# A two-stage kernel (gated linear attention, then a feed-forward layer): low parts and scaled queries on GpSimd, high parts on VectorE

## The chip, the cores and the metric

One core of one Trainium2 chip. The time is the device time of one execution in microseconds; 582.28 us is the median of three executions before the change (582.17, 582.28 and 584.62). The engines are named as in the profile: PE is TensorE's matmuls, PEld its weight loads, DVE VectorE, ACT ScalarE, POOL GpSimd, and SP the engine that issues the loads and stores.

## What is computed

A recurrence over 768 steps for 4 batches of 8 heads of 48 channels, and on its output (3072 tokens of 384 channels) a two-layer feed-forward block with 2048 hidden channels and an activation built from softplus and erf:

```
state = zeros(B, H, D, D)
for t in range(S):
    state = alpha[t][..., None] * state + k[t] outer v[t]
    y[t]  = q[t] @ state
x = y as (B*S, H*D)
h  = x @ w_in
sp = max(h, 0) + log1p(exp(-|h|))
g  = h * erf(sp)
out = g @ w_out
```

## The kernel before

The recurrence is done in 24 chunks of 64 steps for two batches at once. Of a chunk, `ld` issues the loads of alpha, k, q and v on SP; `a1` is the running product A of alpha (one scan on VectorE); `a2` makes 1/A with a logarithm and an exponential on ScalarE and refines it on VectorE; `a3` multiplies: K = k/A (line 175) and the scaled queries Q = q*A (lines 178 to 180), both on VectorE; `a4` transposes K and forms the scores on TensorE; `a5` forms the chunk's output and the new state T on TensorE and VectorE, and puts the output, split in a high and a low part, into x_hi and x_lo. The input tiles raw_a, raw_q and raw_k exist once, so the next `ld` waits until the current chunk has read them.

The feed-forward part works in 12 blocks of 256 tokens, a block being two chunks. The 2048 hidden channels are cut into four groups `g`, and each group into two halves. `H_g_half` is the first product (18 matmuls, TensorE), copied to `hs` by ScalarE. `U` is a tanh, `L1` three logarithms and exponentials, `G` a Gelu on ScalarE, `L2` and `Z` two long VectorE operations each; after `Z` the tile `hs` holds the gated values. `U` and `G` need one table of functions on ScalarE and `L1` and `a2` another; the steps `GELU` and `LN` load them (line 115).

`O_g_half` is the second product (lines 347 to 370). All large products are made in pairs of fp32r numbers: a value is split into a high part, rounded to fp32r, and a low part, the rest. `O` makes the high part `gh` of 512 gated values per partition (on VectorE for the first half of the even groups, 24 in all; on ScalarE for the other 72), then on VectorE the low part `gl` = value - gh, and adds up three products, gh with w_out's high part, gh with its low part, and gl with its high part, for two slices of hidden channels and two halves of the tokens: 12 matmuls into the two accumulators `acc`. `gh` and `gl` have two buffers each. `out` copies the accumulators and stores them.

The weights come in 12 slices of w_in (`wi_n`) and 16 of w_out (`wo_n`); they arrive as 64-bit floats, and VectorE and ScalarE make an fp32 number of each in three VectorE steps and one ScalarE step, and then split it (lines 379 to 404).

The order of all this is written out by hand in three lists of steps (lines 27 to 41): `START` once, for the weights, the first six chunks, the first block's `H` to `L2` and the first `H` of the next block; `ORDER` eleven times, once for each further block, with the second half (`G`, `Z`, `O`) of the block before (`@-1`) and the first `H` of the next (`@1`) woven in; `TAIL` for the second half of the last block. The tile framework orders each engine's queue from these lists by its own priorities; every engine works its queue in order.

Of the kernel before, what the change touches and what calls it, by code (L numbers as in the profile page):

```python
# [15 lines left out]
AF = mybir.ActivationFunctionType  # L16
# [7 lines left out]
LNEXP, GELU = "natural_log_exp_and_others", "gelu_and_others"  # L24
# [2 lines left out]
START, ORDER, TAIL = (  # L27
    z.split()
    for z in (
# [10 lines left out]
    )  # L40
)

# [2 lines left out]
def gla_moe(ctx: ExitStack, tc: tile.TileContext, q, k, v, alpha, w_in, w_out, out):  # L45
    nc = tc.nc
# [3 lines left out]
    P = NI * TC  # L50
    B, H, S = M * NI, 2 * NP, CPB * TC
    W = NP * NI * TC
    NT, DM = out.shape
# [4 lines left out]
    NF = FF // P  # L58
    GT = 4
# [27 lines left out]
    for i in range(NI):  # L87
        half = maskn[i * TC : (i + 1) * TC]
        nc.gpsimd.affine_select(
            out=half, in_=half, pattern=[[1, TC]], compare_op=ALU.is_ge, fill=0.0, base=0, channel_multiplier=-1  # L90
# [16 lines left out]
    wo_hi = const.tile([P, NF, DM], F32R, name="wo_hi")  # L107
    wo_lo = const.tile([P, NF, DM], F32R, name="wo_lo")
# [25 lines left out]
    class Chunk:  # L134
# [37 lines left out]
        def a3(self):  # L172
            flat = "p a i t -> p (a i t)"
            w = self.K.rearrange(flat)
            nc.vector.tensor_tensor(out=w, in0=self.rk.rearrange(flat), in1=w, op=ALU.mult)
            self.Q = at.tile([P, NP, NI, TC], F32, name="Q", tag="Q")
            flat = "p a i t -> p (a i) t"
            nc.vector.tensor_tensor(
                out=self.Q.rearrange(flat), in0=self.rq.rearrange(flat), in1=self.A[:, :, 1:], op=ALU.mult
            )  # L180

# [77 lines left out]
    class Moe:  # L259
# [87 lines left out]
        def O(self, g, half):  # L347
            if g == 0 and half == 0:
                self.acc = [self.pl.acc.tile([P, 512], F32, name="acc", tag="acc") for _ in range(2)]
            sl = slice(half * 512, (half + 1) * 512)  # L350
            gg = self.hs[g][:, sl]
            gh = self.pl.gp.tile([P, 2, TB], F32R, name="gh", tag="gh")
            gl = self.pl.gp.tile([P, 2, TB], F32R, name="gl", tag="gl")
            ghf = gh.rearrange("p a t -> p (a t)")
            if half == 0 and g % 2 == 0:
                nc.vector.tensor_copy(out=ghf, in_=gg)  # L356
            else:
                nc.scalar.activation(ghf, gg, AF.Copy)  # L358
            nc.vector.tensor_tensor(  # L359
                out=gl.rearrange("p a t -> p (a t)"), in0=gg, in1=ghf.bitcast(F32), op=ALU.subtract  # L360
            )
            for u in range(2):
                f = g * GT + half * 2 + u
                for tt in range(2):
                    ts = slice(tt * P, (tt + 1) * P)
                    for n, (gt, wt) in enumerate(((gh, wo_hi), (gh, wo_lo), (gl, wo_hi))):
                        nc.tensor.matmul(  # L367
                            out=self.acc[tt][:, :DM], lhsT=gt[:, u, ts], rhs=wt[:, f, :],
                            start=f == 0 and n == 0, stop=f == NF - 1 and n == 2,
                        )  # L370

        def out(self):
            for tt in range(2):
# [154 lines left out]
    for i in range(1, NBLK):  # L528
# [6 lines left out]
        out=top[:, 0:2], in_=flags.rearrange("p n two -> p two n"), op=ALU.max, axis=mybir.AxisListType.X  # L535
# [67 lines left out]
```

## Time and profile before

| | before |
|---|---|
| median of three executions | 582.28 us |
| the profiled execution, whole | 582.33 us |
| its span, first to last instruction | 580.4 us |
| mean granted clock of TensorE | 0.969 |
| matmuls | 7386 |
| low parts gl, VectorE (line 359) | 96, mean 686 ns |
| high parts gh, ScalarE (line 358) | 72, mean 625 ns |
| high parts gh, VectorE (line 356) | 24, mean 419 ns |
| scaled queries Q, VectorE (line 178) | 24, mean 684 ns |

An instruction's duration in the profile reaches beyond the point at which the next one may start; on a full engine the distance from start to start is what it costs. In rows of the timeline the first number is the start and the second the duration, both in us. In rows of groups the last part is the total of the group in us, the mean of one in ns, and the idle time of the engine just ahead of it with what ended it. In rows of waits stand the total, the number of times and the longest, in us.

### The profile page before, as it was taken

What the parts mean: (1) busy time and instruction counts of PE and PEld (TensorE: products, weight loads), DVE (VectorE), ACT (ScalarE), POOL (GpSimd) and SP (SyncE); (2) the same over time, 40 slices, a digit from 0 to 9 for tenths busy, and PEclk for the clock granted to TensorE, in tenths of its full rate; (3) what the DMA queues carried; (4) which work ended last, traced back from release to release, by engine and by line L of the source; (5) the groups of instructions that cost most, each with busy time, mean ns of one, the idle gap of its engine ahead of it and who ended that gap; (6) DMA issues with size and microseconds to landing.
All of it is one profiled execution on the core that took longest, in us unless ns stands there. A gap on an engine that the chain in (4) does not pass through costs nothing.

```text
span 580.4 us, 16926 instructions
## 1 busy us (share of the span) xinstructions
PE 519.5 (90%) x7386; PEld 496.0 (85%) x7386; DVE 483.6 (83%) x688; ACT 468.6 (81%) x704; POOL 2.4 (0%) x16
## 2 busy tenths in 40 slices
PE   0588687499999999999999999999999999999584
PEld 0486686488989999999999999999999999999584
DVE  6779969999999979969789699699699698594970
ACT  4446799579999799699699798797896996989911
POOL 1000000000000000000000000000000000000000
PEclk9999799789999999999999999999999999999878
DMA  6575633522412222212202312221211100000000
GB/s 194 177 230 168 203 91 107 178 86 63 128 28 61 76 55 62 64 52 75 88 25 65 88 32 72 75 61 43 73 62 44 53 8 30 1 29 1 28 0 33
DMA packets 36370, 43.64 MB, mean 75 GB/s; under 512 B 21952, under 2 KB 25024, under 8 KB 36288
## 3 DMA queue, kind: packets, MB, share of 16 engines
q1 hardware_dynamic: 36288, 42.48, 24.3%
q8 instruction: 60, 0.98, 0.7%
q14 instruction: 22, 0.18, 0.1%
HBM read 37.75 MB, written 4.72 MB: 73 GB/s over the span
## 4 chain that ended last, share of the span: by engine, by line
PE 69%; DVE 15%; ACT 9%; issue 3%; DMA 2%; SPq 0%; ACTq 0%; DVEq 0%
PE acc L367 29%; PE ph L310 29%; PE py L226 4%; PE pS L198 3%; DVE wbuf L401 2%; DVE s L342 2%; ACT s L326 2%; PE pu L237 1%; PE pn L187 1%; DVE wbuf L404 1%; DVE A L156 1%; DVE t L334 1%; DVE w L335 1%; DVE hs L343 1%; ACT hs L315 1%
## 5 line engine op out<-in xcount | busy, mean ns | idle before, releaser
L310 PE MATMUL ph<-x_hi,wi_hi 128*128 128x256 f32 x576 | 166.9, 290 | 7.5 <-ACT wi_hi L379 4.8
L310 PE MATMUL ph<-x_lo,wi_hi 128*128 128x256 f32 x576 | 164.0, 285 | 0.0
L310 PE MATMUL ph<-x_hi,wi_lo 128*128 128x256 f32 x576 | 163.7, 285 | 0.3 <-DVE wi_lo L380 0.2
L367 PE MATMUL acc<-wo_hi,gh 128*128 128x384 f32 x384 | 133.2, 347 | 16.4 <-DVE gh L356 16.4
L367 PE MATMUL acc<-wo_hi,gl 128*128 128x384 f32 x384 | 131.4, 346 | 2.0 <-DVE gl L359 1.9
L367 PE MATMUL acc<-wo_lo,gh 128*128 128x384 f32 x384 | 131.0, 341 | 0.0
L310 PEld LDWEIGHTS ph<-x_hi,wi_hi 128*128 128x128 f32 x576 | 111.4, 194 | 10.1 <-ACT wi_hi L379 5.1
L359 DVE TENSOR_TENSOR gl<-hs,gh 128x512 fp32r<-128x512 f32 x96 | 64.9, 686 | 58.4 <-ACT gh L358 57.6
L310 PEld LDWEIGHTS ph<-x_hi,wi_lo 128*128 128x128 f32 x576 | 111.5, 194 | 1.0 <-DVE wi_lo L380 0.8
L310 PEld LDWEIGHTS ph<-x_lo,wi_hi 128*128 128x128 f32 x576 | 111.0, 193 | 0.5 <-DVE x_lo L275 0.3
L367 PEld LDWEIGHTS acc<-wo_hi,gh 128*128 128x128 f32 x384 | 73.8, 192 | 18.0 <-issue 8.7
L315 ACT ACTIVATE hs<-ph 128x512 f32<-128x512 f32 x96 | 56.3, 590 | 39.3 <-PE ph L310 38.1
L367 PEld LDWEIGHTS acc<-wo_hi,gl 128*128 128x128 f32 x384 | 72.7, 191 | 7.4 <-DVE gl L359 7.0
L367 PEld LDWEIGHTS acc<-wo_lo,gh 128*128 128x128 f32 x384 | 73.7, 192 | 0.0
L334 DVE TENSOR_TENSOR t<-s,w 128x1024 f32<-128x1024 f32 x48 | 58.5, 1218 | 1.9 <-ACT w L328 1.4
L335 DVE SCALAR_TENSOR_TENSOR w<-t,w 128x1024 f32<-128x1024 f32 x48 | 58.4, 1216 | 0.3
L358 ACT ACTIVATE gh<-hs 128x512 fp32r<-128x512 f32 x72 | 44.9, 625 | 16.3 <-PE acc L367 12.5
L343 DVE SCALAR_TENSOR_TENSOR hs<-s,hs 128x1024 f32<-128x1024 f32 x48 | 57.9, 1215 | 0.1
L342 DVE TENSOR_TENSOR s<-s,w 128x1024 f32<-128x1024 f32 x48 | 57.5, 1215 | 0.4 <-ACT s L338 0.4
L326 ACT ACTIVATE s<-s,fixed 128x1024 f32<-128x1024 f32 x48 | 54.6, 1141 | 0.0
L321 ACT ACTIVATE s<-hs 128x1024 f32<-128x1024 f32 x48 | 49.7, 1055 | 1.6 <-DVE wbuf L398 0.9
L328 ACT ACTIVATE w<-w 128x1024 f32<-128x1024 f32 x48 | 50.4, 1051 | 0.3
(62 smaller groups left out, 715.1 us busy)
## 6 DMA issues: line engine op xcount, KB each, us to landing
raw_v<-in_v_dram SPq DMA_DIRECT2D x24, 448.0 KB, 3.7
wst<-in_moe_w_in_dram SPq DMA_DIRECT2D x12, 512.0 KB, 5.7
wst<-in_moe_w_out_dram SPq DMA_DIRECT2D x16, 384.0 KB, 3.7
raw_a<-in_alpha_dram SPq DMA_DIRECT2D x48, 96.0 KB, 2.9
raw_k<-in_k_dram SPq DMA_DIRECT2D x48, 96.0 KB, 2.2
raw_q<-in_q_dram SPq DMA_DIRECT2D x48, 96.0 KB, 2.3
out_dram<-o SPq DMA_DIRECT2D x24, 192.0 KB, 1.9
```

The lines of the kernel that those rows point to most:

```text
L310: nc.tensor.matmul(out=o, lhsT=wt[:, kt, fs], rhs=xt[:, kt, :], start=n == 0, stop=n == 3 * KT - 1)
L315: nc.scalar.activation(self.hs[g][:, sl], ph, AF.Copy)
L321: tab(nc.scalar.activation(self.s[g], self.hs[g], AF.Tanh, scale=-0.5))
L326: tab(nc.scalar.activation(s, s, AF.Ln, scale=0.5 - 2.0**-24, bias=bhalf))
L328: tab(nc.scalar.activation(w, w, AF.Exp, scale=-1.0))
L334: nc.vector.tensor_tensor(out=t, in0=s, in1=w, op=ALU.mult)
L335: nc.vector.scalar_tensor_tensor(out=w, in0=t, scalar=2.0, in1=w, op0=ALU.add, op1=ALU.mult)
L342: nc.vector.tensor_tensor(out=s, in0=s, in1=w, op=ALU.mult)
L343: nc.vector.scalar_tensor_tensor(out=h, in0=s, scalar=RT2 / 2, in1=h, op0=ALU.subtract, op1=ALU.mult)
L358: nc.scalar.activation(ghf, gg, AF.Copy)
L359: nc.vector.tensor_tensor(out=gl.rearrange("p a t -> p (a t)"), in0=gg, in1=ghf.bitcast(F32), op=ALU.subtract)
L367: nc.tensor.matmul(out=self.acc[tt][:, :DM], lhsT=gt[:, u, ts], rhs=wt[:, f, :], start=f == 0 and n == 0, stop=f == NF - 1 and n == 2,)
```

## The change

The scaled queries of `a3` and the low parts of `O` are made by GpSimd. All 96 high parts are made by VectorE, none by ScalarE. In `O` the eight products with the high part come first and the four with the low part last. The three lists of steps are written anew.

```diff
             self.Q = at.tile([P, NP, NI, TC], F32, name="Q", tag="Q")
-            nc.vector.tensor_tensor(
+            nc.gpsimd.tensor_tensor(
                 out=self.Q.rearrange(flat), in0=self.rq.rearrange(flat), in1=self.A[:, :, 1:], op=ALU.mult
             )
...
-            if half == 0 and g % 2 == 0:
-                nc.vector.tensor_copy(out=ghf, in_=gg)
-            else:
-                nc.scalar.activation(ghf, gg, AF.Copy)
-            nc.vector.tensor_tensor(
+            nc.vector.tensor_copy(out=ghf, in_=gg)
+            nc.gpsimd.tensor_tensor(
                 out=gl.rearrange("p a t -> p (a t)"), in0=gg, in1=ghf.bitcast(F32), op=ALU.subtract
             )
-            for u in range(2):
-                f = g * GT + half * 2 + u
-                for tt in range(2):
-                    ts = slice(tt * P, (tt + 1) * P)
-                    for n, (gt, wt) in enumerate(((gh, wo_hi), (gh, wo_lo), (gl, wo_hi))):
-                        nc.tensor.matmul(
-                            out=self.acc[tt][:, :DM], lhsT=gt[:, u, ts], rhs=wt[:, f, :],
-                            start=f == 0 and n == 0, stop=f == NF - 1 and n == 2,
-                        )
+            for gt, wts in ((gh, (wo_hi, wo_lo)), (gl, (wo_hi,))):
+                for u in range(2):
+                    f = g * GT + half * 2 + u
+                    for tt in range(2):
+                        for wt in wts:
+                            nc.tensor.matmul(
+                                out=self.acc[tt][:, :DM], lhsT=gt[:, u, tt * P : (tt + 1) * P], rhs=wt[:, f, :],
+                                start=f == 0 and wt is wo_hi and gt is gh, stop=f == NF - 1 and gt is gl,
+                            )
```

Of the lists, the beginning of the one for a further block:

```diff
-        "GELU a1_0 G_0@-1 G_1@-1 Z_0@-1 H_3_0 G_2@-1 U_0 H_3_1 Z_1@-1 O_0_0@-1 U_2 O_0_1@-1 O_1_0@-1 G_3@-1 U_1 "
+        "GELU H_3_0 U_1 G_1@-1 U_0 H_3_1 G_3@-1 Z_1@-1 G_0@-1 U_2 Z_0@-1 O_0_0@-1 a1_0 G_2@-1 O_0_1@-1 Z_2@-1 "
```

Lines behind line 358 stand three earlier in the changed kernel: the cast on VectorE is line 355, the low part line 356, the output product line 364.

VectorE's queue in the third block, from the state's update to the second of the two chunks' K, before:

```order
L178 TENSOR_TENSOR Q<-raw_q,A 128x512
L255 TENSOR_TENSOR T<-T,A 128x8x48
L156 SCALAR_TENSOR_TENSOR A<-raw_a,lower 128x520
L178 TENSOR_TENSOR Q<-raw_q,A 128x512
L359 TENSOR_TENSOR gl<-hs,gh 128x512 x2
L169 TENSOR_TENSOR K<-A,r 128x512
L359 TENSOR_TENSOR gl<-hs,gh 128x512
L170 SCALAR_TENSOR_TENSOR K<-K,r 128x512
L175 TENSOR_TENSOR K<-raw_k,K 128x512
L356 CAST gh<-hs 128x512
L359 TENSOR_TENSOR gl<-hs,gh 128x512
```

The same place in the changed kernel, VectorE:

```order
L255 TENSOR_TENSOR T<-T,A 128x8x48
L156 SCALAR_TENSOR_TENSOR A<-raw_a,lower 128x520
L355 CAST gh<-hs 128x512 x3
L169 TENSOR_TENSOR K<-A,r 128x512
L170 SCALAR_TENSOR_TENSOR K<-K,r 128x512
L334 TENSOR_TENSOR t<-s,w 128x1024
L355 CAST gh<-hs 128x512
L175 TENSOR_TENSOR K<-raw_k,K 128x512
```

And GpSimd's queue in the changed kernel, from its first query on (before, it has no work after the constants of the start):

```order
L178 TENSOR_TENSOR Q<-raw_q,A 128x512 x7
L356 TENSOR_TENSOR gl<-hs,gh 128x512 x5
L178 TENSOR_TENSOR Q<-raw_q,A 128x512
L356 TENSOR_TENSOR gl<-hs,gh 128x512 x3
L178 TENSOR_TENSOR Q<-raw_q,A 128x512
L356 TENSOR_TENSOR gl<-hs,gh 128x512 x2
```

Queries and low parts have left VectorE for GpSimd's queue, where seven queries stand ahead of the first low part; casts stand in VectorE's queue where low parts stood.

TensorE's queue at one whole `O`, before:

```order
L367 MATMUL acc<-wo_hi,gh 128x384
L367 MATMUL acc<-wo_lo,gh 128x384
L367 MATMUL acc<-wo_hi,gl 128x384
L367 MATMUL acc<-wo_hi,gh 128x384
L367 MATMUL acc<-wo_lo,gh 128x384
L367 MATMUL acc<-wo_hi,gl 128x384
```

and in the changed kernel:

```order
L364 MATMUL acc<-wo_hi,gh 128x384
L364 MATMUL acc<-wo_lo,gh 128x384
L364 MATMUL acc<-wo_hi,gh 128x384
L364 MATMUL acc<-wo_lo,gh 128x384
L364 MATMUL acc<-wo_hi,gh 128x384
L364 MATMUL acc<-wo_lo,gh 128x384
L364 MATMUL acc<-wo_hi,gh 128x384
L364 MATMUL acc<-wo_lo,gh 128x384
L364 MATMUL acc<-wo_hi,gl 128x384 x4
```

The four products with the low part have moved behind all eight with the high part (of the order before, half an `O` is shown; the other half is the same).

ScalarE's queue in the last block, from the load of the logarithms' table on, before (s and w are the tiles of `L1`, o is the output's copy):

```order
L115 ACT_TABLE_LOAD
L358 ACTIVATE gh<-hs 128x512
L326 ACTIVATE s<-s,fixed 128x1024
L358 ACTIVATE gh<-hs 128x512
L327 ACTIVATE w<-s 128x1024
L326 ACTIVATE s<-s,fixed 128x1024
L358 ACTIVATE gh<-hs 128x512
L328 ACTIVATE w<-w 128x1024
L327 ACTIVATE w<-s 128x1024
L326 ACTIVATE s<-s,fixed 128x1024
L358 ACTIVATE gh<-hs 128x512
L328 ACTIVATE w<-w 128x1024
```

and in the changed kernel, to the end of the core's work:

```order
L115 ACT_TABLE_LOAD
L326 ACTIVATE s<-s,fixed 128x1024 x2
L327 ACTIVATE w<-s 128x1024 x2
L328 ACTIVATE w<-w 128x1024 x2
L326 ACTIVATE s<-s,fixed 128x1024 x2
L327 ACTIVATE w<-s 128x1024 x2
L328 ACTIVATE w<-w 128x1024 x2
L115 ACT_TABLE_LOAD
L338 ACTIVATE s<-s 128x1024
L372 ACTIVATE o<-acc 128x384
L338 ACTIVATE s<-s 128x1024 x3
L372 ACTIVATE o<-acc 128x384 x3
```

The casts have left ScalarE's queue, and the first output copy stands behind the second table load instead of ahead of it.

18 rows, old and new, of the table RT2 are left out of this document.

## The prediction

> **What bounds the kernel now.** I read the busy line of the page first, then the busy times by stage, then the waits of TensorE.
>
> ```profile
> PE 519.5 (90%) x7386; PEld 496.0 (85%) x7386; DVE 483.6 (83%) x688; ACT 468.6 (81%) x704; POOL 2.4 (0%) x16
> ...
> 0.00:80.00 80.00, 50.65 (x913) 45.69 (x914) 62.14 (x116) 45.38 (x85) 2.41 (x16) 0.96 0.60 186
> 80.00:115.00 35.00, 22.22 (x489) 19.90 (x488) 33.26 (x56) 29.60 (x50) 0.00 (x0) 0.89 0.40 125
> 115.00:164.00 49.00, 46.88 (x635) 43.63 (x636) 48.46 (x77) 44.47 (x69) 0.00 (x0) 0.94 0.30 88
> 164.00:520.00 356.00, 355.82 (x5094) 344.51 (x5094) 304.98 (x403) 316.01 (x461) 0.00 (x0) 1.00 0.18 53
> 520.00:545.00 25.00, 24.86 (x164) 24.05 (x162) 16.53 (x19) 22.04 (x28) 0.00 (x0) 1.00 0.02 9
> 545.00:580.40 35.40, 19.03 (x96) 18.24 (x96) 18.22 (x22) 11.09 (x15) 0.00 (x0) 0.78 0.07 25
> ```
>
> The columns of a stage are its length, the busy time of PE, PEld, DVE, ACT and POOL, the granted clock and the DMA share. The whole-span shares (90, 83, 81%) hide three different kernels. From 164 to 520 us TensorE is busy 355.82 of 356 us: there it is the limit, and nothing taken from VectorE or ScalarE shortens those 356 us. From 80 to 115 us VectorE is busy 33.26 of 35 us while TensorE has 22.22: VectorE is the limit. From 115 to 164 us both are nearly full (48.46 and 46.88 of 49). After 545 us TensorE has 19.03 of 35.4 us and both others are half idle: that is a chain.
>
> ```profile
> DVE gl L359 <- ACT gh L358: 57.6, 26, 7.1
> ...
> PE acc L367 <- DVE gh L356: 16.4, 2, 8.6
> ```
>
> So the time has two handles: how early TensorE becomes full (about 164 us), and how long it stands still at the end. The second row shows TensorE's two long waits for a high part, 16.4 us together; one is before the first output product at 115 us, the other (8.6) in the tail. The 57.6 us in which VectorE waits for ScalarE's high parts lie mostly under a full TensorE and are worth nothing by themselves.
>
> **The start.** The steps from one start to the next on a busy VectorE are the price of an instruction there:
>
> ```profile
> 113.41 0.55 DVE L380 TENSOR_TENSOR wo_lo<-wbuf,wo_hi 128x384 fp32r<-128x384 f32 x1
> 113.88 0.55 DVE L404 SCALAR_TENSOR_TENSOR wbuf<-wbuf 128x384 int32<-128x384 int32 x1
> 114.35 0.35 DVE L398 TENSOR_SCALAR wbuf<-wst 128x384 int32<-128x384 int32 x1
> 114.62 0.42 DVE L356 CAST gh<-hs 128x512 fp32r<-128x512 f32 x1
> 114.95 0.55 DVE L401 SCALAR_TENSOR_TENSOR wbuf<-wbuf 128x384 int32<-128x384 int32 x1
> 115.42 0.55 DVE L380 TENSOR_TENSOR wo_lo<-wbuf,wo_hi 128x384 fp32r<-128x384 f32 x1
> ...
> 161.52 0.42 DVE L356 CAST gh<-hs 128x512 fp32r<-128x512 f32 x1
> ...
> 298.37 0.69 DVE L359 TENSOR_TENSOR gl<-hs,gh 128x512 fp32r<-128x512 f32 x1
> 298.97 1.22 DVE L335 SCALAR_TENSOR_TENSOR w<-t,w 128x1024 f32<-128x1024 f32 x1
> ...
> 323.29 0.68 DVE L178 TENSOR_TENSOR Q<-raw_q,A 128x512 f32<-128x512 f32 x1
> 323.89 1.22 DVE L343 SCALAR_TENSOR_TENSOR hs<-s,hs 128x1024 f32<-128x1024 f32 x1
> ```
>
> A high-part cast costs VectorE 0.33 us (114.62 to 114.95), a low part 0.60 (298.37 to 298.97), a scaled query 0.60 (323.29 to 323.89). The row at 161.52 is the first cast of the second block: from the products behind it on, TensorE is full. Ahead of it VectorE's order holds 9 queries, 8 low parts and 2 casts; in the changed order, ahead of the first cast of that block, it holds none, none and 8. That is -9 x 0.60 - 8 x 0.60 + 6 x 0.33 = **-8.2 us** of VectorE's work, in a stretch where VectorE was full for the last 80 us of it.
>
> TensorE may not be able to take all of this, since it also waits at the first output product (cast at 114.62). Ahead of that cast 6 queries go (-3.6), but one more slice of w_out stands there (0.47 three times and 0.27, +1.7): -1.9 us. Between the two casts TensorE had 2.1 us of idle time to give back (49 less 46.88), so this path gives at least 1.9 + 2.1 = 4.0. The new start order can move the 17.9 us in which VectorE is idle in the first 80 us either way; the last slice of w_in comes earlier in VectorE's order, which speaks for earlier. I take **-6.0 us**, between 4.0 and 8.2.
>
> **The steady part** I cost at nothing. Per block ScalarE loses 6 casts, VectorE loses 8 low parts and 2 queries and gains 6 casts; the cover is TensorE's 355.82 of 356. TensorE's own work is the same matmuls in another order:
>
> ```profile
> 306.39 0.34 PE L367 MATMUL acc<-wo_lo,gh 128*128 128x384 f32 x1
> 306.56 0.34 PE L367 MATMUL acc<-wo_hi,gl 128*128 128x384 f32 x1
> 306.74 0.34 PE L367 MATMUL acc<-wo_hi,gh 128*128 128x384 f32 x1
> 306.91 0.34 PE L367 MATMUL acc<-wo_lo,gh 128*128 128x384 f32 x1
> ```
>
> Every step is 0.17 us, whether the next matmul keeps the accumulator (hi, lo, low) or changes it (306.56 to 306.74), so the new order costs nothing. It buys cover: eight products with the high part, 8 x 0.17 = 1.4 us, now stand ahead of the first that needs the low part.
>
> **What GpSimd's part costs** no row shows. The nearest ones:
>
> ```profile
> L128 POOL MEMSET T<- 128x512 f32 x1 | 0.5, 524 | 0.0
> ...
> masks.py:199 POOL TENSOR_SCALAR_AFFINE_SELECT ident<-ident 128x128 f32<-128x128 f32 x1 | 0.3, 292 | 0.1
> masks.py:197 POOL MEMSET ident<- 128x128 f32 x1 | 0.2, 204 | 0.3 <-POOLq L562 0.3
> ```
>
> Writing 512 elements takes 0.52 us: the lower bound. Reading one operand of 128 adds 292 - 204 = 88 ns, so two operands of 512 add 8 x 88 = 0.70: **1.23 us**, my estimate. The upper bound is the same with the reading at twice that price, 1.93 us. At 1.23 us a low part fits inside the 1.4 us of cover even if its cast ends only just before the products begin, and TensorE spends 12 x 0.17 = 2.1 us on each piece, so even six pieces in a row leave GpSimd time; at 1.93 us it still keeps pace but each first piece could wait 0.5 us. Two buffers let the cast and the low part run a piece ahead. A new wait stands behind each cast on TensorE (all its later work queues behind the first low product) and one on VectorE (a cast waits until TensorE has freed a high-part buffer, with the next block's work behind it); the second takes the place of the 57.6 us row, and is hidden by the same full TensorE. On GpSimd a query ahead of low parts can hold them up while it waits for its load. The reload of raw_q now waits on GpSimd, and what SP issues behind it waits too; the DMA share of 0.18 in the steady stage is the cover.
>
> The Trainium skill, "GPSIMD Engine Reference", section Performance versus the Vector engine, gives 4497 ns for a two-input add of 2048 elements; a quarter of it is an estimate of 1.12 us, which would change no term here.
>
> **The tail.**
>
> ```profile
> 529.48 1.28 ACT L115 ACT_TABLE_LOAD   x1
> 530.77 0.63 ACT L358 ACTIVATE gh<-hs 128x512 fp32r<-128x512 f32 x1
> 531.31 1.14 ACT L326 ACTIVATE s<-s,fixed 128x1024 f32<-128x1024 f32 x1
> ...
> 540.73 0.62 ACT L358 ACTIVATE gh<-hs 128x512 fp32r<-128x512 f32 x1
> 541.25 1.05 ACT L328 ACTIVATE w<-w 128x1024 f32<-128x1024 f32 x1
> ...
> 545.77 1.28 ACT L115 ACT_TABLE_LOAD   x1
> ```
>
> ```profile
> 544.67 0.19 PE L541 MATMUL pf<-fixed,count 128*1 128x1 f32 x2
> 553.46 0.66 PE L367 MATMUL acc<-wo_hi,gh 128*128 128x384 f32 x1 [8.59 <-DVE gh L356]
> ```
>
> In the last block ScalarE is full from the table load at 529.48 to the one at 545.77, and TensorE runs dry at 544.67 because the gated values come 8.6 us later. Of those 16.3 us six are casts of 0.52 to 0.54 (530.77 to 531.31, 540.73 to 541.25), 3.2 us, and one an output copy that the changed order puts behind the load. TensorE's part up to there is the same. What comes next, VectorE's chain from the last logarithm to the first cast, holds six long operations in both orders. So **-3.2 us**; the bounds are -1.6 (half of it, if ScalarE's steps, now in pairs of equal ones, wait for each other) and -4.0 (with the output copy). The low parts on GpSimd (1.23 against TensorE's 2.1 per piece) do not slow the eight pieces that follow.
>
> **Sum**, against the profiled execution's own 582.33 us (span 580.4 and 1.93 around it; the median of the runs shown is 582.28, so no correction): 582.3 - 6.0 - 3.2 = **573.1 us**. Its own range, from the bounds of both terms, is 570 to 577, and 567 if the start order also fills VectorE's early gaps.
>
> **Rivals.** (1) *GpSimd stops VectorE.* If VectorE's operations with two SBUF inputs and GpSimd's cannot run at once, each GpSimd operation takes its 1.23 us out of VectorE. Up to the second block's first cast there are 17; six fall among VectorE's 17.9 idle us, the other 11 cost 13.5 us against 8.2 saved: +5.3. In the steady part one block is the distance of these rows:
>
> ```profile
> 288.91 1.28 ACT L115 ACT_TABLE_LOAD   x1
> ...
> 330.33 1.28 ACT L115 ACT_TABLE_LOAD   x1
> ```
>
> In 41.4 us VectorE is busy 41.4 x 304.98 / 356 = 35.5 us; less 10 x 0.60, plus 6 x 0.33, 31.5. With 10 x 1.23 on top it is 43.8, over the limit by 2.4; if GpSimd runs inside the waits of VectorE (57.6 us over some 11 blocks, 5.2 each) it is 38.6 and under it. I take a third, 0.8 us in each of 8.6 periods: +7. With the tail's -3.2 this gives 582.3 + 5.3 + 7 - 3.2 = **591 us**, slower. It decides as soon as the lost time passes the 9.9 us that VectorE gets back each 41.4 (41.4 - 31.5). For it: almost all of VectorE's long work reads two SBUF tiles. Against it no row speaks: GpSimd worked only in the first 3 us, beside memsets. The Trainium skill states this rule, in "SBUF — State Buffer", section Who interferes with whom: a VectorE instruction with two SBUF inputs contends with a GpSimd one that reads SBUF, through an exclusive lock under which the other fully blocks. By that rule this rival would be the forecast; no run here shows it yet. Chance 0.25.
>
> (2) *Half of it.* The two slow each other only partly, or low parts come late now and then (0.5 us on some 20 first pieces is 10 us), and eat the gain: **582 us**, no change. Chance 0.18.
>
> (3) *The start does not follow VectorE.* ScalarE is busy 29.60 of 35 and 44.47 of 49 us there, the loads and the half clock (0.89) also have a say; then only the tail counts: 582.3 - 3.2 = **579.1 us**. Chance 0.12, half of it on either side of the bound.
>
> That the change does not do what it says I leave without a chance: the order shows GpSimd's low parts and queries and no cast on ScalarE.
>
> **The numbers.** A difference of 0.5% (2.9 us) is about what a measurement of this kernel can tell from none. The forecast of 573 has 0.45. Faster: 0.45 + 0.06 = 0.51; same: 0.18 + 0.06 = 0.24; slower: 0.25. The range goes from 567 to 592: below it lies a tenth of the forecast's case, above it half of rival 1's, together under 0.2.
>
> **What would show it.**
>
> ```profile
> L343 DVE SCALAR_TENSOR_TENSOR hs<-s,hs 128x1024 f32<-128x1024 f32 x48 | 57.9, 1215 | 0.1
> L342 DVE TENSOR_TENSOR s<-s,w 128x1024 f32<-128x1024 f32 x48 | 57.5, 1215 | 0.4 <-ACT s L338 0.4
> ```
>
> In the profile of the changed kernel: TensorE full from about 158 us on rather than 164; VectorE's long operations still at 1215 ns (rival 1: longer, in step with GpSimd's work); GpSimd's two kinds at about 1.2 us; no wait of TensorE for a low part among the long ones; the last wait for a high part near 5 us rather than 8.6. A period of 41.4 us that grows proves the steady part wrong, and with it the forecast.

## The result and the profile after

The changed kernel takes **616.99 us** (median of four executions, 616.67 to 620.09) against 582.24 us for the kernel before on the same chip: a ratio of 1.0609, 95% interval 1.0567 to 1.065. It is 6% slower; the forecast was 573 and the range 567 to 592. The profiled execution spans 618.3 us. One execution among all that follow, the profiled one of e4b below (623.47 us), fell in a slower state of the chip, and e4b's time and ratio below are those of its other three.

The busy line of its page:

```profile
PE 527.7 (85%) x7386; PEld 503.0 (81%) x7386; DVE 507.6 (82%) x640; ACT 433.0 (70%) x632; POOL 216.6 (35%) x136
```

VectorE has 48 instructions fewer than before and 24 us more of busy time (507.6 against 483.6). The groups of instructions of VectorE and GpSimd show why, first in the changed kernel, then three of them before:

```profile
L343 DVE SCALAR_TENSOR_TENSOR hs<-s,hs 128x1024 f32<-128x1024 f32 x48 | 72.5, 1524 | 0.1
L335 DVE SCALAR_TENSOR_TENSOR w<-t,w 128x1024 f32<-128x1024 f32 x48 | 70.1, 1461 | 0.7
L169 DVE TENSOR_TENSOR K<-A,r 128x512 f32<-128x512 f32 x24 | 27.3, 1136 | 7.4 <-ACT r L166 7.4
L203 DVE TENSOR_TENSOR sT<-pS,maskn 128x512 f32<-128x512 f32 x24 | 16.3, 681 | 2.9 <-PE pS L198 2.8
L275 DVE TENSOR_TENSOR x_lo<-py,x_hi 128x192 fp32r<-128x192 f32 x48 | 14.9, 346 | 0.2 <-ACT x_hi L274 0.2
L356 POOL TENSOR_TENSOR gl<-hs,gh 128x512 fp32r<-128x512 f32 x96 | 172.0, 1798 | 174.0 <-DVE gh L355 129.9 <-PE acc L364 41.6 <-ACT s L321 1.6
L178 POOL TENSOR_TENSOR Q<-raw_q,A 128x512 f32<-128x512 f32 x24 | 42.3, 1760 | 216.4 <-DVE A L156 180.9 <-DMA raw_q<-in_q_dram 15.6 <-PE ph L310 12.7
```

```profile
L169 DVE TENSOR_TENSOR K<-A,r 128x512 f32<-128x512 f32 x24 | 16.6, 690 | 6.0 <-ACT r L166 6.0
L203 DVE TENSOR_TENSOR sT<-pS,maskn 128x512 f32<-128x512 f32 x24 | 16.4, 682 | 1.3 <-PE pS L198 1.3
L275 DVE TENSOR_TENSOR x_lo<-py,x_hi 128x192 fp32r<-128x192 f32 x48 | 15.0, 348 | 3.1 <-ACT x_hi L274 3.1
```

The long operations at L343 were 1215 ns and are 1524; L169 was 690 and is 1136. Operations with one input in PSUM, the memory that TensorE writes its results to (pS, py), have not changed: L203 was 682, L275 348. A low part on GpSimd that does not have to wait for VectorE takes close to what was estimated (next view: 1.32 us); the mean is 1.80.

A piece of the steady part, VectorE, GpSimd and TensorE by the timeline (start, duration):

```profile
342.68 1.20 DVE L343 SCALAR_TENSOR_TENSOR hs<-s,hs 128x1024 f32<-128x1024 f32 x1
342.89 3.16 POOL L178 TENSOR_TENSOR Q<-raw_q,A 128x512 f32<-128x512 f32 x1 [12.28 <-DVE A L156]
343.79 1.22 DVE L342 TENSOR_TENSOR s<-s,w 128x1024 f32<-128x1024 f32 x1
344.93 0.68 DVE L203 TENSOR_TENSOR sT<-pS,maskn 128x512 f32<-128x512 f32 x1
345.53 1.14 DVE L355 CAST gh<-hs 128x512 fp32r<-128x512 f32 x2
345.66 0.35 PE L226 MATMUL py<-sT,raw_v 64*32 64x64 f32 x16 [1.12 <-DVE sT L203]
346.48 1.32 POOL L356 TENSOR_TENSOR gl<-hs,gh 128x512 fp32r<-128x512 f32 x1 [0.43 <-DVE gh L355]
...
346.48 3.56 POOL L356 TENSOR_TENSOR gl<-hs,gh 128x512 fp32r<-128x512 f32 x2 [0.43 <-DVE gh L355]
346.59 4.52 DVE L343 SCALAR_TENSOR_TENSOR hs<-s,hs 128x1024 f32<-128x1024 f32 x2
```

(The row at 346.48 stands twice, before and after the next low part is merged into it.) Both kinds of blocking are here. GpSimd's low part starts at 346.48, and VectorE's two operations from 346.59 on take 4.52 us, where two such rows take 2.35 undisturbed. The other way round, the query at 342.89 comes while VectorE is in its own operations; it ends at 346.05, that is 1.1 us after VectorE has turned to the operation on PSUM at 344.93. VectorE's operations up to that one have their normal lengths, so there GpSimd is the one that waits; of the two casts behind it (1.14 us for 0.33 + 0.42) the first is held until the query is done. And TensorE stood still for sT, which VectorE made 1.12 us late: earlier in its queue, at 317.61, 321.29, 325.00 and 329.98, four operations of the same kinds had each taken 0.5 to 1.1 us more than usual.

TensorE's waits in the whole span (total, times, longest), and two windows of two steady periods each (length, then busy PE, PEld, DVE, ACT, POOL, clock, DMA), the second from experiment e3 below, in which GpSimd does nothing:

```profile
PE acc L364 <- DVE gh L355: 22.1, 3, 11.2
PE py L226 <- DVE sT L203: 12.4, 10, 2.2
PE acc L364 <- POOL gl L356: 8.7, 5, 5.4
```

```profile
312.30:399.60 87.30, 84.28 (x1267) 80.38 (x1266) 77.43 (x89) 66.69 (x98) 35.93 (x21) 1.00 0.21 60
```

```profile
286.80:369.50 82.70, 82.70 (x1266) 80.65 (x1265) 76.02 (x109) 67.24 (x97) 0.00 (x0) 1.00 0.21 62
```

With GpSimd idle TensorE is busy for all of its 82.70 us. In the changed kernel it has 3.0 us of idle time in two periods, and they are 4.6 us longer; the other 1.6 us stand as longer busy time of TensorE for the same matmuls (84.28), and why is not shown. VectorE is not full there (77.43 of 87.30): it is late at one place in its order, and TensorE waits at that place.

The first low part of all and the tail:

```profile
120.08 9.44 POOL L356 TENSOR_TENSOR gl<-hs,gh 128x512 fp32r<-128x512 f32 x2 [11.85 <-DVE gh L355]
128.34 1.65 PE L364 MATMUL acc<-wo_hi,gl 128*128 128x384 f32 x4 [5.42 <-POOL gl L356]
...
563.75 1.28 ACT L115 ACT_TABLE_LOAD   x1
576.92 1.28 ACT L115 ACT_TABLE_LOAD   x1
587.47 0.66 PE L364 MATMUL acc<-wo_hi,gh 128*128 128x384 f32 x1 [7.55 <-DVE gh L355]
587.49 5.93 POOL L356 TENSOR_TENSOR gl<-hs,gh 128x512 fp32r<-128x512 f32 x2 [8.72 <-DVE gh L355]
592.24 1.65 PE L364 MATMUL acc<-wo_hi,gl 128*128 128x384 f32 x4 [1.87 <-POOL gl L356]
```

The first two low parts take 9.44 us (8.21 of it the first) instead of 2.6, and TensorE waits 5.42 us for the first of them.

### The profile page after: what moved, and what is told of

The parts are those of the page before. It is cut to its first block, busy times and chain, and to the rows that moved or that the text cites. A ratio compares the mean times of both kernels' runs of the same rounds, so it can differ in the third digit from the quotient of the medians.

```text
span 618.3 us, 17096 instructions
## 1 busy us (share of the span) xinstructions
PE 527.7 (85%) x7386; PEld 503.0 (81%) x7386; DVE 507.6 (82%) x640; ACT 433.0 (70%) x632; POOL 216.6 (35%) x136
## 4 chain that ended last, share of the span: by engine, by line
DVE 33%; ACT 19%; PE 18%; issue 9%; POOL 5%; DMA 3%; SPq 0%; DVEq 0%; POOLq 0%; ACTq 0%
PE acc L364 9%; PE ph L310 8%; DVE t L334 8%; DVE w L335 5%; DVE s L342 4%; DVE K L169 3%; DMA out_dram<-o 3%; POOL gl L356 3%; ACT s L338 2%; ACT hs L315 2%; ACT w L327 2%; ACT s L326 2%; DVE A L156 2%; DVE hs L343 2%; ACT L115 2%
## 5 line engine op out<-in xcount | busy, mean ns | idle before, releaser
L356 POOL TENSOR_TENSOR gl<-hs,gh 128x512 fp32r<-128x512 f32 x96 | 172.0, 1798 | 174.0 <-DVE gh L355 129.9
L310 PEld LDWEIGHTS ph<-x_hi,wi_hi 128*128 128x128 f32 x576 | 111.6, 194 | 10.8 <-ACT wi_hi L376 5.2
L178 POOL TENSOR_TENSOR Q<-raw_q,A 128x512 f32<-128x512 f32 x24 | 42.3, 1760 | 216.4 <-DVE A L156 180.9
L355 DVE CAST gh<-hs 128x512 fp32r<-128x512 f32 x96 | 46.4, 494 | 67.1 <-PE acc L364 57.7
L364 PE MATMUL acc<-wo_hi,gl 128*128 128x384 f32 x384 | 87.2, 351 | 9.4 <-POOL gl L356 8.7
L343 DVE SCALAR_TENSOR_TENSOR hs<-s,hs 128x1024 f32<-128x1024 f32 x48 | 72.5, 1524 | 0.1
L335 DVE SCALAR_TENSOR_TENSOR w<-t,w 128x1024 f32<-128x1024 f32 x48 | 70.1, 1461 | 0.7
L334 DVE TENSOR_TENSOR t<-s,w 128x1024 f32<-128x1024 f32 x48 | 65.5, 1364 | 2.8 <-ACT w L328 1.2
L342 DVE TENSOR_TENSOR s<-s,w 128x1024 f32<-128x1024 f32 x48 | 62.7, 1323 | 0.1
L338 ACT ACTIVATE s<-s 128x1024 f32<-128x1024 f32 x48 | 49.4, 1057 | 12.4 <-DVE t L334 12.3
L372 ACT ACTIVATE o<-acc 128x384 f32<-128x384 f32 x24 | 11.7, 486 | 60.2 <-PE acc L364 32.0
```

The lines of the kernel that those rows point to most:

```text
L178: nc.gpsimd.tensor_tensor(out=self.Q.rearrange(flat), in0=self.rq.rearrange(flat), in1=self.A[:, :, 1:], op=ALU.mult)
L310: nc.tensor.matmul(out=o, lhsT=wt[:, kt, fs], rhs=xt[:, kt, :], start=n == 0, stop=n == 3 * KT - 1)
L334: nc.vector.tensor_tensor(out=t, in0=s, in1=w, op=ALU.mult)
L335: nc.vector.scalar_tensor_tensor(out=w, in0=t, scalar=2.0, in1=w, op0=ALU.add, op1=ALU.mult)
L338: tab(nc.scalar.activation(self.s[g], self.s[g], AF.Gelu, scale=-RT2))
L342: nc.vector.tensor_tensor(out=s, in0=s, in1=w, op=ALU.mult)
```

## The experiments

**Theory A**: GpSimd's operations and VectorE's on SBUF, the on-chip memory in which the tiles of GpSimd's operations and of most of VectorE's lie, cannot run at once; each holds the other up. **Theory B**: the low part simply comes late, because one more engine stands between the cast and the product. **Theory C**: the new lists and the casts on VectorE cost the time, not GpSimd.

### Which part of the change: e1, e2, e3, e6

All are the changed kernel with one thing put back.

```diff
 e1 (low parts back), e2 (queries back), e3 (both back)
-            nc.gpsimd.tensor_tensor(
+            nc.vector.tensor_tensor(
 e6: START, ORDER, TAIL of before
```

> The changed kernel, with only the scaled queries on GpSimd; the low parts are back on VectorE, the lists and the casts as changed. Theory A (a GpSimd operation with two inputs holds VectorE's long operations up for as long as it runs, and is held up by them): 24 of the 120 GpSimd operations are left, so about a fifth of the lengthening of VectorE's work stays: mean of the products at L343 near 1.28 us rather than 1.52; time 583 to 595. Theory B (VectorE's lengthening costs nothing by itself; the low part comes late to TensorE because one more engine stands between the cast and the product): no low part crosses to GpSimd any more, so the whole loss goes: 573 to 583. Theory C (the new lists and the casts on VectorE cost it): 605 or more.

> The changed kernel, with only the low parts on GpSimd; the queries are back on VectorE. Theory A: 96 of 120 GpSimd operations are left: VectorE's L343 near 1.47 us, time 605 to 620. Theory B: all the waits for low parts stay, and VectorE has 24 products more: 612 to 625. If the queries alone did the harm (they meet the K operations of the next chunks): below 595.

> The changed kernel with GpSimd idle: queries and low parts on VectorE, all casts on VectorE, the lists and TensorE's order as changed. Theories A and B: VectorE's operations have the lengths of before (L343 1.215 us); the time is that of before with 6 casts a block moved from ScalarE to VectorE, 578 to 590. Theory C (lists and casts): 605 or more.

> The changed kernel with the lists of before: engines, casts and TensorE's order as changed. The run without GpSimd work has shown the rest of the change to be worth -6; if the lists carry that, this is 618 to 626; if they carry nothing, 614 to 620; if the new lists are made for GpSimd's place in the chain, above 626.

| | us | ratio to before | 95% interval |
|---|---|---|---|
| e3: GpSimd idle | 576.29 | 0.9887 | 0.9852 to 0.9922 |
| e1: queries on GpSimd | 581.4 | 0.9975 | 0.9949 to 1.0002 |
| e2: low parts on GpSimd | 609.62 | 1.0476 | 1.044 to 1.0513 |
| after: both | 616.99 | 1.0609 | 1.0567 to 1.065 |
| e6: both, old lists | 613.58 | 1.0508 | 1.0466 to 1.055 |

Without GpSimd's part the change gains 1.1%; GpSimd's part costs 616.99 - 576.29 = 40.7 us, the queries alone 5.1, the low parts alone 33.3. Theory C falls: without GpSimd the new lists and casts are no loss, and the lists of before make the changed kernel only about 1% faster by the two ratios (e6, a little under all three of its ranges).

Theory A did not get everything right. e1's time lies in the range of theory B, not in that of A: the expected lengthening of the L343 group (1.28 us) did not come, it stayed at 1213 ns, and it was the 24 queries that were stretched, to a mean of 2068 ns. TensorE has no wait for GpSimd in e1 either; where its 5.1 us come from is open. e2's time lies in A's range, but its lengthening is not at L343 (1276 ns, expected 1.47 us); it is at L335 (1454), at the scan of L156 (1525, usually 1234) and at L169 (1052). e3 came out 2 us below its range.

In e3 the moved work is back on VectorE, in these groups of its page:

```profile
PE 513.1 (89%) x7386; PEld 494.3 (86%) x7386; DVE 508.0 (88%) x760; ACT 433.7 (75%) x632; POOL 2.4 (0%) x16
...
L356 DVE TENSOR_TENSOR gl<-hs,gh 128x512 fp32r<-128x512 f32 x96 | 64.9, 685 | 6.2 <-PE acc L364 6.1
L178 DVE TENSOR_TENSOR Q<-raw_q,A 128x512 f32<-128x512 f32 x24 | 16.5, 687 | 1.3 <-DMA raw_q<-in_q_dram 1.0
```

This gives the account of VectorE. The change takes 120 operations from it, at 0.60 us from start to start 72 us (the totals above, 64.9 and 16.5, hold the overlap of neighbours too). Yet it was busy 507.6 us instead of 508.0. The durations of the operations that it kept add up to 70 us more than in e3, the most of it at L343 (14.9), L335 (11.7), L169 (10.8), L170 (7.9), and at L334 and the casts (6.9 each). Nearly all that it had handed over came back.

### Work that nobody waits for: e4, e4b, e4c, e5

The kernel before, with its own lists and all its work on VectorE, and beside each low part and each query a piece of GpSimd work on a tile that no other engine uses. A one-column operation on the same input sets its place. To make room, the output's copy shares the place of the tile r.

```diff
+    free = const.tile([P, 401], F32, name="free")
 behind each low part (behind each query, with A in gg's place)
+            nc.gpsimd.tensor_tensor(out=free[:, :1], in0=gg[:, :1], in1=gg[:, :1], op=ALU.subtract)
+            for w in (400, 112):
+                nc.gpsimd.tensor_tensor(out=free[:, :w], in0=free[:, :w], in1=free[:, :w], op=ALU.mult)
 e4c: tensor_copy(out=free[:, :w], in_=lower[:, :w]) in the loop
 e5: three memset(free[:, :400], 1.0) in the loop's place
 e4: the one-column operation writes a column that the products don't read
```

> The kernel before, with GpSimd work that nobody waits for: beside each low part and each query a one-column operation that paces it, and two in-place products of 400 and 112 columns on a tile that only GpSimd uses (about 1.3 us). The output's copy uses the place of the tile r. Theory A: VectorE's long operations lengthen from 1.215 to 1.4 us or more, and the time rises to 592 to 620, though no engine waits for GpSimd. Theory B: VectorE's operations keep their lengths, 581 to 585. Theory C: 581 to 585.

> As e4, with each free-standing pair of products made to follow its one-column operation (which now writes a column that the products read), so that GpSimd's work lies beside the low parts and the queries and not all at the start. 120 pairs of some 1.3 us, as the changed kernel has 120 operations, and still nobody waits for a result of theirs. Theory A: the cost is VectorE's: L343's like lengthen to 1.4 us or more, and the time is 592 to 612. Theory B (the cost is the low part's way to TensorE): 581 to 586.

> As e4b, with three fills of 400 columns (about 0.42 us each by the start's fill of 520, 0.53 us) in place of the two products, so that GpSimd writes and does not read. Theory A in its narrow form (GpSimd's reads meet VectorE's): 581 to 585, VectorE's operations at their lengths of before. In its wide form (any GpSimd work in SBUF holds VectorE): as e4b.

> As e4b, with copies of 400 and 112 columns (one input, one output) in place of the products of two inputs. If a GpSimd operation holds VectorE only with two inputs to read: as the fills, 584 to 588, VectorE's long operations at 1.215 us. If any GpSimd read does: between fills and products, 595 to 615.

| | us | ratio | 95% interval |
|---|---|---|---|
| e4: products, not paced | 683.37 | 1.1739 | 1.17 to 1.1778 |
| e4b: products, paced | 614.17 | 1.0539 | 1.0494 to 1.0584 |
| e4c: copies, paced | 593.71 | 1.0157 | 1.0106 to 1.0209 |
| e5: fills, paced | 586.49 | 1.0065 | 1.0037 to 1.0093 |

e4 does not answer the question: its products hung on nothing, the framework moved all of them into the first 220 us, and the one-column operations behind them kept tiles from being freed (ScalarE once waited 43.8 us for one). Its loss, far above every range, is that of another order of work. e4b is the same with the products held in place. Nobody waits for its products, and it loses nearly what the changed kernel lost, 2 us more than theory A's range allowed. From the groups of e4b:

```profile
L349 DVE SCALAR_TENSOR_TENSOR hs<-s,hs 128x1024 f32<-128x1024 f32 x48 | 63.3, 1327 | 0.2
L281 DVE TENSOR_TENSOR x_lo<-py,x_hi 128x192 fp32r<-128x192 f32 x48 | 15.0, 347 | 5.3 <-ACT x_hi L280 5.3
```

and of e5, the same lines with fills:

```profile
L349 DVE SCALAR_TENSOR_TENSOR hs<-s,hs 128x1024 f32<-128x1024 f32 x48 | 57.9, 1215 | 0.2
L362 DVE CAST gh<-hs 128x512 fp32r<-128x512 f32 x24 | 11.2, 465 | 0.7 <-PE acc L376 0.7
L370 POOL MEMSET free<- 128x400 f32 x288 | 125.6, 436 | 16.7
```

Fills keep GpSimd as long (three of 0.436, 1.31 us), come out 1.5 us over the narrow range, and leave VectorE's two-input operations at 1215 ns; of these groups only the cast is touched (465, before 419). Copies, with one input to read, lie between: L349's group is at 1271 ns, midway, and the time nearer to the fills, below the range for "any read" and above that for "two inputs". The one-column operations are in e5 as in e4b. What they hold is not quite the same, since in e4b they also wait behind slower products: ScalarE waits 12.1 us for them in e4b's whole span and 4.2 in e5's, too little to make the loss. So it is GpSimd's reading that meets VectorE's, and the theory in its narrow form holds. The Trainium skill states this in "SBUF — State Buffer", section Who interferes with whom: a VectorE instruction with two SBUF inputs contends with a GpSimd one that reads SBUF, not with one that only writes it. The 1327 ns of e4b, the 1215 of e5 and the 347 of the operation with an input in PSUM agree with it line by line.

A one-column operation of e4b shows how long GpSimd can be kept out (timeline, VectorE and GpSimd):

```profile
303.31 8.24 POOL L368 TENSOR_TENSOR free<-hs 128x1 f32<-128x1 f32 x1 [13.38 <-DVE hs L349]
309.14 2.35 DVE L349 SCALAR_TENSOR_TENSOR hs<-s,hs 128x1024 f32<-128x1024 f32 x2
311.41 0.61 DVE L281 TENSOR_TENSOR x_lo<-py,x_hi 128x192 fp32r<-128x192 f32 x2
```

Elsewhere in this run the shortest of its kind takes 0.19 us. Here it takes 8.24: VectorE goes from one SBUF operation to the next without a gap until, at 311.41, it reads PSUM, and GpSimd's operation ends at 311.55.

### The way of the low part, and the reads, in the changed lists: e12, e11

e12 is the changed kernel with one column of each low part and query, and fills for the rest; what waits for what is the same. e11 is e3 with the free-standing products of e4b.

```diff
 e12, likewise for Q
-            nc.gpsimd.tensor_tensor(
-                out=gl.rearrange("p a t -> p (a t)"), in0=gg, in1=ghf.bitcast(F32), op=ALU.subtract
-            )
+            nc.gpsimd.tensor_tensor(out=gl2[:, :1], in0=gg[:, :1], in1=ghf[:, :1].bitcast(F32), op=ALU.subtract)
+            for _ in range(2):
+                nc.gpsimd.memset(gl2.bitcast(F32), 2.0**-10)
```

> The changed kernel with each low part and each query on GpSimd replaced by one column of it and two fills of the tile with a constant (together some 1.2 us, like the operation itself, and waited for and queued in the same way); low parts and queries are left out of what is computed. Theory A (GpSimd's reads and VectorE's get in each other's way): the loss goes, VectorE's L343 at 1.215 us, 565 to 580. Theory B (one engine more on the way to TensorE): the loss stays, 605 to 620. Both: in proportion between.

> The run without GpSimd work (576.3), with the free-standing pairs of products of e4b beside each low part and each query, for which nobody waits; VectorE does all of its own work. Theory A: 605 to 625. Theory B: 575 to 582.

e12 took 588.6 us (1.0098, interval 1.0065 to 1.0131), e11 630.1 (1.0788, 1.0732 to 1.0843), 5 us over theory A's range and far from B's. Both theories said something else of e12: the loss neither went nor stayed; 12.3 us over e3 are left of 40.7. VectorE is at its normal lengths in it (the group of L343 at 1210 ns; the casts, 453 against 422 in e3, are a little longer) and busy for 443.1 us instead of 507.6. The starts of ScalarE's table loads, one at the same place of each kernel's work, show where the rest lies (us from the span's start):

| | before | after | e3 (GpSimd idle) | e12 (fills) | after - e3 | e12 - e3 |
|---|---|---|---|---|---|---|
| Gelu's load, first block | 99.0 | 105.9 | 100.6 | 102.1 | 5.3 | 1.5 |
| logarithms' load, third block | 167.1 | 177.4 | 163.9 | 173.0 | 13.5 | 9.1 |
| the same, sixth block | 288.9 | 312.3 | 286.8 | 296.2 | 25.5 | 9.4 |
| the same, last block | 529.5 | 563.7 | 525.9 | 535.4 | 37.8 | 9.5 |
| end of the span | 580.4 | 618.3 | 575.3 | 586.8 | 43.0 | 11.5 |

In the steady six periods from the sixth block's load to the last one's, the changed kernel loses 12.3 us to e3 and e12 nothing: what it costs there that the low part comes by way of GpSimd is nothing, as long as GpSimd hardly reads. These six periods side by side (us; the granted clock is 1.00 in all of them):

| | length | TensorE busy | VectorE busy | GpSimd busy |
|---|---|---|---|---|
| before | 240.6 | 240.6 | 199.6 | 0 |
| e3: GpSimd idle | 239.1 | 239.1 | 212.1 | 0 |
| e12: low parts as fills | 239.1 | 239.1 | 181.2 | 95.8 |
| e5: before, with free-standing fills | 240.1 | 240.1 | 200.0 | 98.5 |
| after | 251.4 | 242.8 | 212.0 | 100.8 |
| e4b: before, with free-standing products | 251.8 | 242.5 | 231.6 | 156.5 |

GpSimd is as busy in e12 and in e5 as after the change, and TensorE stays full; e4b, whose products nobody waits for, loses as much as the changed kernel. In this stage only the reading is left as the cause. Of the 25.5 us up to the sixth block's load, 9.4 stay with fills, and of the tail's 5.2, 2.0. Even these aren't all the way's length, for e12 still reads one column each time (timeline of e12):

```profile
165.21 4.07 POOL L360 TENSOR_TENSOR gl<-hs,gh 128x1 fp32r<-128x1 f32 x1 [8.99 <-DVE gh L358]
165.45 0.42 DVE L358 CAST gh<-hs 128x512 fp32r<-128x512 f32 x1
165.78 2.35 DVE L346 SCALAR_TENSOR_TENSOR hs<-s,hs 128x1024 f32<-128x1024 f32 x2
168.06 1.23 DVE L156 TENSOR_TENSOR_SCAN A<-raw_a,lower 128x520 f32<-128x520 f32 x1
169.31 0.83 DVE L358 CAST gh<-hs 128x512 fp32r<-128x512 f32 x1
```

One column is kept out for 4.07 us by a cast, two products and a scan; at 170.65 TensorE has waited 3.24 us for the low part behind it. How the 11.5 us divide between such lock-outs and plain length stays open.

### Where e3's gain comes from: e7, e8, e9, e10

```diff
 e7: the kernel before with the new lists; e8: before with TensorE's new order
 e9: e8, and all casts on VectorE (the lists of before)
 e10: e3, with the casts of the first three blocks shared as before
```

> The kernel before with the lists of the change and nothing else. If the lists carry the gain of the run without GpSimd work: 575 to 578; if the casts on VectorE or TensorE's order carry it: 580 to 585, as the casts on ScalarE stand ahead of the logarithms in the tail.

> The kernel before with TensorE's order of the change (all products of a step with the high part ahead of those with the low part) and nothing else. By the prediction's sum it costs nothing (0.17 us a product either way) and gives TensorE up to 0.7 us more before it needs a low part: 581 to 583. If the run without GpSimd work owes its gain to it: 576 to 579.

> The kernel before with TensorE's order of the change and all casts on VectorE; GpSimd idle, the lists of before. The new lists alone gave +0.4%, so if the casts carry the gain of the run without GpSimd work (ScalarE's casts stand ahead of the logarithms and of the next load of a table): 575 to 580, the tail's logarithms to Gelu load near 13.2 us. If only casts and new lists together give it: 582 to 588, as VectorE has 6 casts of 0.42 us more in each block of the start.

> The kernel without GpSimd work (new lists, new order), with the casts of the first three blocks shared as before, 6 of 8 on ScalarE, and all casts on VectorE only from the fourth block on. If VectorE is what bounds the start: up to 3 x 6 x 0.42 = 7.6 us less of VectorE work there, half of it worth something: 570 to 575. If ScalarE's casts there hold the table loads back, as in the tail: 577 to 582.

The new lists alone: 585.74 us, ratio 1.0037 (1.0017 to 1.0057). TensorE's order alone: 582.14, 0.9946 (0.9922 to 0.997). Order and casts on the lists of before: 580.63, 0.9936 (0.9909 to 0.9963). e10: 578.79, 0.9899 (0.987 to 0.9928). The gain of e3 is no single part's: the order seems to give half of it, the casts add nothing that can be told from it on the old lists, and the new lists, a small loss alone, seem to pay once the casts have left ScalarE (0.9887 against 0.9936, intervals that overlap a little, so this is not shown). Sharing the casts in the start changes nothing measurable. Why the order alone gains 0.5% isn't shown: the spans of the profiled executions are 580.5 and 580.4, and the executions of the kernel before in that round lie between 581.25 and 586.38, wider apart than the gain. e7 and e9 came out just outside their ranges. **e3 has the lowest time of all runs**: the change without GpSimd.

## Why the prediction was wrong, step by step

- **The start, -6.0 us.** It failed in its first premise, that work off VectorE is time won on VectorE: 72 us left it and 70 us of lengthening came back. The row that the prediction read, the first cast of the second block, came at 171.43 us instead of 161.52 before, 9.9 later where 6.0 earlier was forecast. In e3, without GpSimd, it came at 159.6.
- **The steady part at nothing, covered by a full TensorE.** The failing step of the sum. From the third block's load to the last one's (167.1 to 529.5 before, 177.4 to 563.7 after), a stretch in which TensorE was full before, the change costs 386.3 - 362.4 = 23.9 us: 13.1 up to the sixth block's load and 251.4 - 240.6 = 10.8 in the six periods behind it. The cover was read as if TensorE's busy time were a fixed property of the stage; it is full only while what VectorE makes for it comes in time (sT in the changed kernel's steady rows, the low parts in e4b's), and e4b takes that away with work that is hardly in anybody's way but VectorE's.
- **GpSimd's price, 1.23 us, between 0.52 and 1.93.** Right for the operation alone (1.32 in the timeline). Among VectorE's operations the means, 1.80 and 1.76, are still inside the bounds, but single ones are not (up to 8.21), and neither bound held what such an operation does to VectorE. "1.4 us of cover" rested on the price alone.
- **TensorE's order at no cost.** Right; e8 shows no loss.
- **The tail, -3.2 us.** The term itself came: from the logarithms' load to Gelu's it was 16.3 us and is 13.2 (563.75 to 576.92). What comes behind it was taken as unchanged and went from 34.6 us to 41.4: in the rows of the tail, TensorE waits 7.55 us for a high part (5 were foreseen) and then 1.87 for a low part that took 4.69 us among VectorE's operations. In e3, without GpSimd, the whole tail from the load on is 49.4 us instead of 50.9.
- **Rival 1 was the mechanism, with too small a chance and too small a price.** It had 0.25 and 591 us. Its start (+5.3) was 10.3 by the third block's load; its 7 us of the steady part were 23.9, and its 0.8 us a period still 1.8 in the last six (10.8); its tail of -3.2 was 580.4 - 529.5 = 50.9 going to 54.6, +3.7. The three make up the 37.9 us between the two spans. Its price counted only what GpSimd takes from VectorE's total, and let it decide "as soon as the lost time passes the 9.9 us" that VectorE gets back. VectorE had idle time left when the period grew. What decides is whether one result on TensorE's path (sT, gh, gl) lies behind a blocked operation; and that VectorE also keeps GpSimd out was left out of the price altogether.
- **"Against it no row speaks"**, the prediction said. No row spoke for the forecast either, since before the change GpSimd never works beside VectorE's products, and the one statement at hand, that of the Trainium skill ("SBUF — State Buffer", Who interferes with whom), spoke for the rival, with almost all of VectorE's long work of the kind it names. That should have made rival 1 the likeliest; it was given a quarter because no run had shown it.

## What to carry to other kernels

Moving elementwise operations with SBUF inputs from VectorE to GpSimd freed next to nothing here (70 of 72 us came back), since most of VectorE's own work reads two SBUF tiles: before such a move, count the two engines as one resource, in which the moved operation has also become twice as long (1.32 us against 0.69). With the 24 queries alone (e1) some 5 of 14 us came back, so how much depends on where the operations fall. A cheap test before such a move is to put the same operations on GpSimd with no one waiting for them, held in place by a dependence, and to look at the mean of VectorE's groups; fills in their place give the cost of the way alone. "The engine isn't the bound there" is no cover where a full engine depends, operation by operation, on the order in which the slowed one delivers.

## What was not expected of the hardware

Who has to wait is not simply who comes second for one operation. Where VectorE's operations follow each other without a gap, a waiting GpSimd operation can be kept out through many of them: a one-column operation, 0.19 us at its shortest, took 8.24, and the first of the changed kernel's low parts, at 8.21, held up TensorE by 5.42 us, while VectorE ran at its normal lengths. In these cases GpSimd got in where VectorE read PSUM or had a gap. Casts and the scan kept it out as well as the two-input products (the rows of e12 at 165.45 and 168.06).

But that is not the rule. Of the changed kernel's 96 low parts 4 took over 3 us, and the median is 1.59; in the rows from 346.48 on the two engines take turns, GpSimd's two operations with 1.32 and 2.28 us, VectorE's with 2.29 and 2.31. What decides between the two cases is not shown.
